# An S4 convolution and a PEER expert layer on one core: parameters in three parts, step sizes on chip, gelu for two head groups, and a new order

## The chip, the cores and the metric

The kernel runs on one core of a Trainium2 chip. A core has five engines with queues of their own: PE (TensorE, matrix products; its weight loads are shown as PEld), DVE (VectorE), ACT (ScalarE), POOL (GpSimd) and SP (SyncE, which here only issues DMAs). Engines work at the same time and wait for one another through semaphores; each runs its own instructions strictly in order. The metric is the device time of one execution in microseconds (us); the median of several runs counts.

## The reference, cut to what matters

```python
xn = layernorm(x)                                  # x: 1 x 2048 x 448, no affine part
out = x + s4(xn) + peer(xn)

def s4(u):                                         # 448 channels, 256 states each
    dt = exp(log_dt)[:, None]
    A, B, C = A_re + 1j*A_im, B_re + 1j*B_im, C_re + 1j*C_im
    P = exp((dt * A)[:, :, None] * arange(2048))
    K = einsum("dn,dnl,dn->dl", C, P, dt * B).real # a filter of 2048 taps for each channel
    return causal_convolution(u, K) + u * Dskip    # by FFT in the reference

def peer(x):                                       # 16 heads, 64 x 64 = 4096 experts
    q = einsum("nd,dhc->nhc", x, w_q)              # two halves of 256 for each head
    s1, s2 = q[..., :256] @ k1.T, q[..., 256:] @ k2.T
    e = 64 * argmax(s1) + argmax(s2)               # top 1 of each half
    g = softmax(top score over one candidate)
    return sum over heads of g * gelu(x . u[e]) * v[e]
```

## The kernel before

**The work.** The 2048 tokens are 16 tiles of 128. Four kinds of work have no data in common until the end, and run beside each other:

- *Parameters* (`params`, and `exp32` for the step sizes). `exp32` computes dt = exp(log_dt) in 19 DVE operations on a tile of 112x4; the result goes to memory (`dt_d`) and comes back broadcast to 128 partitions. `params` takes six tables (real and imaginary parts of A, B and C, states on the partitions, 2 x 448 columns = 896) and makes from them, for each channel and state, a log magnitude and a phase, as tables of exponents and of integer phase steps. Both tables go to memory (`tt_d`, `tp_d`) and are loaded back for four batches at a time (`exponents`, `steps`). It is a chain of 36 DVE operations on 128x896, four on POOL, and some on ACT (sine, square, logarithm, exponential) between them.
- *The filter* (`batch`, `products`): 56 batches of 8 channels. For each, PE makes exponents (lg, L579), ACT exponentiates them (mg, L590), DVE makes phases (ph, L610 and L614), ACT takes sines and cosines (CS, L629 to L635), DVE multiplies (zi and mg, L660 to L666), PE sums over the states (kp, L682). After each quarter of the channels `conv` convolves the tokens with the filter by matmuls and leaves the result in memory (t_d).
- *The router* (`combine`, `ln`, `score`). `combine` multiplies w_q with the keys (32 loads wq, products wc, L862, transposed by wt, L875). `ln` normalizes the tiles (L915 to L921), transposes them (xtp, L943) and projects them (up, L724). `score` makes for each tile and four groups of heads the scores in PSUM (sc, L961 and L970, banks of the pool s2), reduces them to the maximum (mx, L985, DVE, 64 of these), finds its position and writes the indices ig.
- *The experts* (`experts`): for each tile four groups of 4 heads of 32 tokens x 4. POOL gathers rows of u and v (ue, L1083, four gathers for a group), DVE takes dot products with the token (L1091), and a chain between ACT and DVE makes gelu: square (ACT, L1098), x (DVE, L1101), dw (DVE, L1110), tanh (ACT, L1104), th (DVE, L1107), and A, the 32-column selector times th (DVE, L1114). PE adds up v rows with A (po, L1121). There are 64 such chains. `final` adds everything into the output (L1167).

**What sets the order.** Nothing is scheduled by a planner: the string `ORDER` has a character for each step of each stream (`CODE` maps characters to streams), and steps are emitted in that order; each engine's queue is what falls to it. Buffers are rings: gathers, wq loads and scratch tiles share the ring `q` ("ue", eleven of them), score banks are "s2", po has one bank.

## Time and profile before

| | us |
|---|---|
| three runs | 761.42, 763.97, 760.34 |
| median | 761.42 |
| profiled execution | 763.02 |
| its span, first to last instruction | 761.1 |
| ACT busy | 552.9 |
| POOL busy | 360.7 |

The profile is of one execution. Busy times are of instructions that compute; issuing a DMA or waiting is not among them. A row of the timeline has the start, the duration, the engine, the line, the operation, the tile written and those read, the shapes, and in brackets the idle time before it with what ended that. A group of instructions has busy time, the mean in ns, and the idle time before its members. Waits are listed as the engine, the tile and line, what was waited for, the total in us, the count and the longest one. An operation's duration includes a tail that the next one on the engine overlaps, so cost is better read from the distance between starts.

Three more things of the trace of before are needed to follow the next part. The first reduction of scores that has a filter product behind it, the 17th, starts at 134.70 us. The last one starts at 357.95, and the last product of the filter ends near 714.6.

### The profile page before, as it was taken

The page shows a single profiled execution, that of the slowest core. Times are in us where ns is not written, and L with a number is a line of the kernel's source. Part 1 is how long each engine was busy: PE and PEld are TensorE (multiplying, and loading weights), DVE is VectorE, ACT ScalarE, POOL GpSimd, SP SyncE. Part 2 cuts the span into 40 slices and gives each one's busy share as a digit, 9 for nine tenths or more (in the row PEclk, how much of TensorE's full clock was granted, in tenths as well). Part 3 has the DMA queues.
Part 4 walks back from the last instruction along what each step waited for, and adds up shares of the span by engine and source line. Part 5 has one row for each costly group of instructions (what it writes and reads, how often), then busy time and mean ns, then how long its engine had stood idle before and what let it go on. Part 6 is the DMA issues. An engine that isn't in the chain of part 4 may idle for free.

```text
span 761.1 us, 19861 instructions
## 1 busy us (share of the span) xinstructions
PE 652.1 (86%) x7628; PEld 355.8 (47%) x7628; DVE 669.5 (88%) x1691; ACT 552.9 (73%) x1137; POOL 360.7 (47%) x307
## 2 busy tenths in 40 slices
PE   1999999999999999999887958679996587899882
PEld 0344333443444444444465734346763344576751
DVE  4896578999999999999999999999998999999840
ACT  3886147566876886774796898888898888999630
POOL 2011024544363645655447686484564657752523
PEclk9999999999999999999999877688987756999995
DMA  9998656978687896887989999899898999977998
GB/s 324 328 374 305 228 136 254 355 238 246 221 257 266 252 327 191 309 255 257 337 300 340 281 324 361 263 327 279 265 342 271 308 325 286 339 248 209 296 178 128
DMA packets 119095, 211.83 MB, mean 278 GB/s; under 512 B 38937, under 2 KB 94233, under 8 KB 118937
## 3 DMA queue, kind: packets, MB, share of 16 engines
q0 software_dynamic: 31232, 124.80, 51.6%
q1 hardware_dynamic: 87768, 85.77, 35.2%
q8 instruction: 60, 0.98, 0.5%
q14 instruction: 35, 0.28, 0.1%
HBM read 180.90 MB, written 33.29 MB: 281 GB/s over the span
## 4 chain that ended last, share of the span: by engine, by line
PE 41%; DVE 29%; ACT 14%; DMA 7%; issue 6%; SPq 1%; POOL 1%; POOLq 0%; DVEq 0%; ACTq 0%
PE sc L961 14%; DVE ue L1091 6%; PE U L798 3%; PE po L1121 3%; DVE mg L666 3%; DVE zi L662 3%; DVE ph L614 3%; PE kp L682 3%; PE sc L970 3%; DMA ue<-in_uv_dram,ig 3%; PE ip L830 2%; PE wc L862 2%; PE up L724 2%; ACT CS L629 2%; DMA VU<-vu_d 2%
## 5 line engine op out<-in xcount | busy, mean ns | idle before, releaser
L1083 POOL DMA_INDIRECT ue<-in_uv_dram,ig x256 | 312.6, 1221 | 309.0 <-PE po L1121 72.9
L961 PE MATMUL sc<-W,xt 128*128 128x512 f32 x384 | 180.1, 608 | 2.2 <-ACT xt L946 1.9
L1091 DVE SCALAR_TENSOR_TENSOR ue<-ue,xr 128x448 f32<-128x448 f32 x256 | 154.1, 617 | 4.0 <-DMA ue<-in_uv_dram,ig 4.0
L961 PEld LDWEIGHTS sc<-W,xt 128*128 128x128 f32 x384 | 69.7, 191 | 91.9 <-issue 83.9
L1121 PE MATMUL po<-ue,A 128*32 128x448 f32 x512 | 68.6, 616 | 9.4 <-DVE A L1114 5.0
L590 ACT ACTIVATE mg<-lg 128x512 f32<-128x512 f32 x112 | 63.4, 600 | 11.1 <-PE lg L579 10.6
L682 PE MATMUL kp<-mg 128*32 128x64 f32 x1792 | 62.3, 237 | 7.9 <-DVE kt L693 3.1
L666 DVE TENSOR_TENSOR mg<-mg,CS 128x1024 f32<-128x1024 f32 x56 | 68.2, 1217 | 0.0
L662 DVE TENSOR_TENSOR zi<-mg,CS 128x1024 f32<-128x1024 f32 x56 | 68.2, 1217 | 0.0
L635 ACT ACTIVATE CS<-CS,halfpi 128x1024 f32<-128x1024 f32 x56 | 64.5, 1152 | 0.8
L614 DVE CUSTOM_DVE_ANT_0 ph<-st,ph 128x512 uint16<-128x512 uint16 (+2 forms) x84 | 64.9, 772 | 0.2
L629 ACT ACTIVATE CS<-ph 128x1024 f32<-128x1024 int32 x56 | 62.6, 1118 | 1.4 <-issue 0.5
L632 ACT ACTIVATE CS<-ph 128x1024 f32<-128x1024 int32 x56 | 63.2, 1128 | 0.0
L682 PE MATMUL kp<-zi 128*32 128x64 f32 x1792 | 61.6, 234 | 0.0
L682 PEld LDWEIGHTS kp<-mg 128*32 128x32 f32 x1792 | 45.2, 119 | 29.2 <-issue 11.7
L579 PE MATMUL lg<-lc,rt 32*128 32x512 f32 x112 | 39.8, 548 | 21.5 <-ACT mg L590 17.5
L702 PE MATMUL vp<-f,kt 128*64 128x128 f32 x448 | 43.6, 326 | 16.5 <-ACT tl L1163 5.0
L985 DVE TENSOR_REDUCE mx<-sc 128x8 f32<-128x512 f32 x64 | 43.6, 682 | 14.6 <-PE sc L970 9.2
L682 PEld LDWEIGHTS kp<-zi 128*32 128x32 f32 x1792 | 47.2, 121 | 0.1
L798 PE MATMUL U<-VU,g 128*64 128x128 f32 x384 | 42.3, 301 | 5.4 <-DVE cp L808 2.7
L702 PEld LDWEIGHTS vp<-f,kt 128*64 128x64 f32 x448 | 28.9, 160 | 38.3 <-issue 11.9
L862 PE MATMUL wc<-wq,kk 128*64 128x448 f32 x128 | 31.7, 586 | 17.1 <-DMA wq<-in_wq_dram 17.1
(244 smaller groups left out, 1242.2 us busy)
## 6 DMA issues: line engine op xcount, KB each, us to landing
wq<-in_wq_dram SPq DMA_DIRECT2D x32, 448.0 KB
xr<-xn_d SPq DMA_DIRECT2D x64, 224.0 KB
vu_d<-vst SPq DMA_DIRECT2D x64, 112.0 KB
VU<-vu_d SPq DMA_DIRECT2D x12, 512.0 KB
t_d<-tq SPq DMA_DIRECT2D x24, 256.0 KB
tl<-t_d SPq DMA_DIRECT2D x12, 512.0 KB
ue<-in_uv_dram,ig POOLq DMA_INDIRECT x256, 6.4
xx<-in_x_dram SPq DMA_DIRECT2D x16, 224.0 KB
```

What stands on the lines that cost most here:

```text
L614: s.nc.vector.tensor_tensor(out=rw(n, 2 * n), in0=rw(0, n), in1=o["st"][:, k, b0:b0 + 2].rearrange("p b h m x -> p (b h m x)")[:, None].to ...
L629: s.nc.scalar.activation(CS[:, 1].rearrange("p (m r x) -> p m r x", r=16, x=2), four(s.ph), AF.Sin, scale=SC)
L635: s.nc.scalar.activation(B["CS"][:, 0], B["CS"][:, 0], AF.Sin, scale=-SC, bias=s.halfpi)
L662: V.tensor_tensor(out=zi[:, 512:], in0=mg[:, 512:], in1=CS[:, 1], op=ALU.mult)
L666: V.tensor_tensor(out=mg[:, 512:], in0=mg[:, 512:], in1=CS[:, 0], op=ALU.mult)
L682: s.nc.tensor.matmul(kp[32 * c:32 * c + 32, 64 * gi:64 * gi + 64], T[ri][:, 1024 + m:1056 + m], view(T[ri], m, [[512, 2], [1, 32]]), start ...
L702: s.nc.tensor.matmul(vp[64 * ri:64 * ri + 64, 128 * gi:128 * gi + 128], B["kt"][:, 64 * gi:64 * gi + 64], s.f1[:, ri], start=True, stop=True)
L798: s.nc.tensor.matmul(U[64 * h:64 * h + 64, sl, ri], s.g[q][:, 2 * kk + h, ri], src[:, k1 + h, :w], start=True, stop=True)
L961: s.nc.tensor.matmul(B["sc", q].rearrange("p a b -> p (a b)"), B["xt"][:, i], w, start=(q % 2 == 0 and i == 0), stop=(q % 2 == 1 and i == 2))
L1083: s.nc.gpsimd.indirect_dma_start(out=ue, out_offset=None, in_=s.io["uv"], in_offset=bass.IndirectOffsetOnAxis(ap=s.IDX[t][:, c, g:g + 1].b ...
L1091: s.nc.vector.scalar_tensor_tensor(Q["ue", c][:, :D], Q["ue", c][:, :D], 1.0, B["xr", c], op0=ALU.mult, op1=ALU.mult, accum_out=Q["dot"][: ...
L1121: s.nc.tensor.matmul(B["po"][32 * c:32 * c + 32, :D], Q["A"][:, c], Q["ue", c][:, D:], start=(g == 0), stop=(g == 3))
```

## The change

Four things change; what is computed stays the same.

1. **Parameters in three parts of channels**, 128, 160 and 160 wide (`PARTS`): 256, 320 and 320 columns where there were 896. Each part has two packed loads (tiles pa and pb) and takes its buffers from the ring `q`. The first part's tables stay on chip: the exponents are transposed straight from the tile pt, and the steps are read from the tile pb (`P["R1"]`). Parts two and three go through memory as before.
2. **Step sizes without memory.** log_dt is broadcast to 128 partitions by its first load, and `exp32` works on 128x448 into the tile `s.dt`, which stays.
3. **Gelu for two groups at once** from tile 4 on (`PT=4`): the tiles x, th and dw become 128x8 and A 128x256, and the four operations of DVE and two of ACT serve eight gathers. 16 + 24 chains take the place of 64.
4. **A new order string**; the mask is loaded later, the DMA scratch is 2048, not 4096.

```diff
+PARTS = (128, 160, 160)
...
 ORDER = (
-    "4HH4HH44441444Z4444H606HH414144114H72III2II72II2I2I7728I8I2IJJ22I2I2I2I72KIZ414I82852I24K4I4COP224C4234LMLDHMHHH4LMDCLM4"
...
+    "013ZHH3HH314Z3353153H33116633HH3H322I2222I2I2II2I2III222I2222I7IJJI3K7IICI7788I2IIL8DC332699I798M7874I77OC8DEC77778I7I9D"
...
-            T["ld"] = s.sm.tile([112, 4], F32, name="ld")
-            s.nc.sync.dma_start(T["ld"], io["log_dt"].rearrange("(p f) -> p f", f=4))
-        x = p.add("c_ld", "SP", xf(112, 16), ldt)
-        ops = s.exp32(T)
-        x = p.chain("c_v", "DVE", ops, deps=[x])
-        x = p.add("dt_st", "SP", xf(112, 16), lambda: s.nc.sync.dma_start(s.dt_d.rearrange("o (p f) -> (o p) f", f=4), T["p"]), deps=[x])
...
+            v, w = s.flat("q", "dq", 1024), s.flat("q", "dr", 1024)
+            T.update(ld=v[:, :D], k=v[:, D:2 * D], r=w[:, :D], ki=w[:, D:2 * D].bitcast(I32), p=s.dt)
+            s.nc.sync.dma_start(T["ld"], io["log_dt"].rearrange("(o f) -> o f", o=1).to_broadcast([128, D]))
+        x = p.add("c_ld", "SP", xf(128, 1792), ldt, take=("ue", "ue"))
+        s.dt_done = p.chain("c_v", "DVE", s.exp32(T), deps=[x], give=("ue", "ue"))
...
-    def params(s, part):
+    def params(s, k):
...
-        N = 2 * D
...
+        d0, w = s.parts[k]
+        N, nb, b0 = 2 * w, w // NB, d0 // NB
+        per = 1024 // N
+        keep = k == 0
...
+        P["tp_done"] = [c1] if keep else [stp(0, 0, "A_re", [f2]), stp(0, 1, "T3", [ph]), stp(1, 0, "B_im", [f1]), stp(1, 1, "T1", [c1])]
...
+                s.nc.tensor.transpose(o["ps"][:, t], P["tt"][t][:, i:i + 4].rearrange("p b k -> p (b k)") if P["keep"] else o["tl"][:, t], s.ident)
...
+            if P["keep"]:
+                o["tp"] = P["R1"][:, :, :, i:i + 4]
...
-        for g in range(4):
+        w = 2 if t >= s.o["PT"] else 1
+        for g0 in range(0, 4, w):
...
+                            for k in ("dot", "x2", "th", "dw"):
+                                Q[k] = s.sm.tile([128, 2, 4], F32, name=k, bufs=2)[:, :w]
...
+                A = Q["A"] = s.sm.tile([128, 2, 4, 32], F32, name="A", bufs=2)[:, :w]
+                s.nc.vector.tensor_tensor(out=A.rearrange("p g c k -> p (g c) k"), in0=s.mask[:, None, :].to_broadcast([128, 4 * w, 32]),
+                                          in1=Q["th"].rearrange("p g c -> p (g c)")[:, :, None].to_broadcast([128, 4 * w, 32]), op=ALU.mult)
...
-    nc = bacc.Bacc("TRN2", target_bir_lowering=False, num_devices=1, dynamic_dma_scratch_size=4096)
+    nc = bacc.Bacc("TRN2", target_bir_lowering=False, num_devices=1, dynamic_dma_scratch_size=2048)
```

In what follows a row is one instruction of an engine's queue: line, operation, tile written and tiles read, shape. The changed kernel's lines are about ten higher: mx is L995, wc is L872, up is L734.

DVE before, the end of the parameter chain around the first reduction of scores (mx); pv, pw, px and pz are parameter tiles, ISA is an integer addition:

```order
L496 TENSOR_SCALAR pv<-pw 128x896
L985 TENSOR_REDUCE mx<-sc 128x8
L921 TENSOR_TENSOR q<-m,y 128x2
L497 ISA px<-pw,pv 128x1792
L498 TENSOR_SCALAR pw<-pw 128x896
L992 TENSOR_TENSOR eq<-sc,mx 128x512
L499 ISA pw<-pw 128x1792
```

DVE now, at the first and second reductions of scores; pa, pb and pt are the tiles of the second part:

```order
L995 TENSOR_REDUCE mx<-sc 128x8
L1002 TENSOR_TENSOR eq<-sc,mx 128x512
L470 RECIPROCAL pb<-pb 128x320
L995 TENSOR_REDUCE mx<-sc 128x8
L433 TENSOR_TENSOR pa<-pa,pb 128x320
L462 TENSOR_TENSOR pt<-pb,pt 128x20x8
L433 TENSOR_TENSOR pa<-pa 128x320
L439 SCALAR_TENSOR_TENSOR pa<-pa 128x320
```

Before, all but the last five of the 36 operations of the chain stand ahead of the first reduction. Now the second part's chain stands among them, and the third part's is further on; it ends here, right ahead of the 17th reduction (the ISA rows are its phase tables, L1103 is a dot product):

```order
L496 TENSOR_SCALAR pb<-pb 128x320
L497 ISA pb<-pb 128x640
L1103 SCALAR_TENSOR_TENSOR ue,dot<-ue,xr 128x448
L928 TENSOR_TENSOR q<-y 128x2
L1013 TENSOR_TENSOR eq<-eq 128x32x16
L929 SCALAR_TENSOR_TENSOR q<-q,v 128x2
L1013 TENSOR_TENSOR eq<-eq 128x32x8
L498 TENSOR_SCALAR pb<-pb 128x320
L1016 TENSOR_REDUCE cm<-eq 128x32
L499 ISA pt<-pt,pb 128x640
```

Between the 16th and the 17th reduction stand 52 rows in all.

PE's first rows before (wt are transposes of wc, xtp of a normalized tile, up the projection of tiles):

```order
L862 MATMUL wc<-wq,kk 64x448 x4
L943 MATMUL xtp<-ident,xx 128x128 x4
L943 MATMUL xtp<-ident,xx 64x128
L862 MATMUL wc<-wq,kk 64x448 x4
L724 MATMUL up<-xx,f_92 128x448 x3
```

and now:

```order
L872 MATMUL wc<-wq,kk 64x448 x4
L734 MATMUL up<-xx,f_91 128x448
L872 MATMUL wc<-wq,kk 64x448 x4
L953 MATMUL xtp<-ident,xx 128x128 x4
L953 MATMUL xtp<-ident,xx 64x128
```

The first up has moved ahead of the first transposes, and three in a row have become single ones between the wc.

DVE's first rows now, where the step sizes (dq, dr, dt) and the first tile's layer norm (v, y, q) alternate:

```order
L355 TENSOR_SCALAR dq<-dq 128x448
L358 TENSOR_SCALAR dq<-dq 128x448
L925 TENSOR_SCALAR v<-s 128x2
L359 TENSOR_SCALAR dq<-dq 128x448
L362 SCALAR_TENSOR_TENSOR dr<-dq 128x448
L362 SCALAR_TENSOR_TENSOR dr<-dq,dr 128x448
L358 TENSOR_SCALAR dt<-dr 128x448
L926 TENSOR_SCALAR y<-v 128x2
```

Before, the same operations stood there on 112x4, between parameter operations on 128x896.

More of the change, by code (lines that the diff above doesn't have):

```diff
@@ L425, in params @@
+        held = 3 if keep else 4
+        l1 = p.add("par_ld", "SP", xf(128, 4 * N * per), ld1, take=("ue",))
+        l2 = p.add("par_ld", "SP", xf(128, 4 * N * (6 - per)), ld2, take=("ue",) * (held - 1))
         d1, d2 = dv(N), dv(N, 2)
@@ L513, in exponents @@
-    def exponents(s, g):
+        P["tt_done"] = [ll] if keep else [p.add("par_st", "SP", xf(128, 128 * nb), lambda t=t: s.nc.sync.dma_start(
+            s.tt_d[:, t, b0:b0 + nb], P["tt"][t]), deps=[ll]) for t in range(2)]
+        p.add("par_f", "NONE", 0, lambda: None, deps=[ph, lf, an, ll, f1, c1] + P["tp_done"] + P["tt_done"],
+              give=("ue",) * (1 if keep else held))
+        return P
+    def exponents(s, P, g):
         p = s.p
         o = {}
+        i = 4 * g - P["b0"]
         def l():
```

287 lines of the change are left out of this document (140 added, 147 removed).

## The prediction

> **What bounds the kernel now.** I read the page's busy shares and slices first, then the windows by stage. Of the slices I show VectorE (DVE) and the clock that TensorE (PE) was granted.
>
> ```profile
> PE 652.1 (86%) x7628; PEld 355.8 (47%) x7628; DVE 669.5 (88%) x1691; ACT 552.9 (73%) x1137; POOL 360.7 (47%) x307
> DVE  4896578999999999999999999999998999999840
> PEclk9999999999999999999999877688987756999995
> PE 41%; DVE 29%; ACT 14%; DMA 7%; issue 6%; SPq 1%; POOL 1%; POOLq 0%; DVEq 0%; ACTq 0%
> ```
>
> PE and DVE are within 17 us of one another, and the chain of waits (fourth line) changes between them. An average cannot say which decides, so here are the stages that I cut: up to PE's first work, up to its last starved piece, the parameters' two halves (the fourth stretch ends with the 17th reduction of the scores, the first that has products behind it), and the long middle to the last product, then the end.
>
> ```profile
> core 0: us, PE busy (x) PEld busy (x) DVE busy (x) ACT busy (x) POOL busy (x), PEclk, DMA share, GB/s
> 0.00:16.40 16.40, 0.00 (x0) 0.01 (x1) 6.92 (x9) 6.79 (x17) 4.77 (x17) 1.00 0.89 314
> 16.40:30.20 13.80, 11.34 (x27) 3.47 (x27) 11.98 (x41) 10.55 (x17) 0.00 (x0) 1.00 0.94 320
> 30.20:62.70 32.50, 32.32 (x155) 13.44 (x156) 30.14 (x37) 24.61 (x63) 5.14 (x2) 1.00 1.01 368
> 62.70:134.70 72.00, 70.10 (x230) 28.43 (x226) 46.97 (x110) 33.70 (x94) 15.39 (x14) 1.00 0.66 223
> 134.70:358.60 223.90, 221.63 (x1755) 96.97 (x1748) 219.25 (x595) 157.21 (x351) 111.65 (x94) 1.00 0.80 263
> 358.60:714.60 356.00, 289.80 (x4907) 193.86 (x4906) 341.42 (x860) 308.75 (x565) 211.69 (x172) 0.85 0.94 301
> 714.60:761.10 46.50, 26.90 (x574) 19.62 (x569) 12.78 (x46) 11.30 (x33) 12.06 (x10) 0.78 0.90 177
> ```
>
> From 134.7 to 714.6 DVE is busy 219.25 + 341.42 = 560.7 of 579.9 us (97%), and PE 511.4 (88%). So DVE bounds the middle: what it loses ahead of 134.7 is not made up later, and DVE work taken out of the middle comes off whole. Ahead of 134.7 DVE has slack: its idle time in the first four stretches is 9.5 + 1.8 + 2.4 + 25.0 = 38.7 us, and there PE sets the pace (70.1 of 72.0). The scores come through PE, and the DVE queue's own waits from 62.7 to 134.7 say so:
>
> ```profile
> DVE mx L985 <- PE sc L970: 8.6, 2, 4.4
> DVE mx L985 <- PE sc L961: 5.1, 5, 1.4
> ```
>
> The change touches that slack, and the gelu chains in the middle.
>
> **Term 1, the head: step sizes and parameters.** The prices come from DVE's timeline and groups:
>
> ```profile
> 17.22 1.08 DVE L432 TENSOR_TENSOR pw<-pw 128x896 f32<-128x896 f32 x1
> 18.22 1.08 DVE L432 TENSOR_TENSOR pw<-pw,px 128x896 f32<-128x896 f32 x1
> 132.24 0.15 DVE L1101 SCALAR_TENSOR_TENSOR x<-x,dot 128x4 f32<-128x4 f32 x1
> 132.31 0.16 DVE L1110 TENSOR_TENSOR dw<-dot,ig 128x4 f32<-128x4 f32 x1
> L435 DVE TENSOR_SCALAR pv<-pv 128x896 f32<-128x896 f32 x2 | 1.2, 623 | 0.0
> ```
>
> Back to back, 896 columns take 18.22 − 17.22 = 1.00 us and 4 columns 132.31 − 132.24 = 0.07 us. So an operation costs 0.07 us plus 1.04 ns a column; one with a single tensor operand (623 ns less the 0.08 overlap is 0.54) costs about half as much a column.
>
> - Step sizes: 19 operations on 112x4 become 19 on 128x448. Ten are TENSOR_SCALAR: 0.07 + 448 x 0.52 ns = 0.30 us; nine have two tensors: 0.54. The sum is 3.0 + 4.8 = 7.8, against 19 x 0.07 = 1.3: +6.5 us. The store and reload of dt vanish, two small transfers, and nobody on the path stood behind them.
> - Parameters: 256 + 320 + 320 columns are the same 896, but 36 DVE operations become 105: 69 more by 0.07 is +4.8 us.
> - Position: pricing every DVE row ahead of the 17th reduction in the two orders this way, the changed one has 10.3 us more: 6.5 + 4.8, less 1.0 of dot products and layer norm that now come later.
> - Idle: parameters used to fill the start, where DVE waits for PE anyway. Now a first part runs ahead of the first reduction, 21.9 us of work in all, and the scores for it are there at about 48 (PE's time up to then in its own row lengths), so about 24 idle; then about 10 more up to the second, whose scores PE has some 13 us later. That is 33.4 us against 38.7, −5.3.
> - Port: a POOL operation of the parameters held DVE up.
>
> ```profile
> 41.81 2.36 POOL L432 TENSOR_TENSOR pv<-pv,dt 128x896 f32<-128x896 f32 x1 [26.85 <-DMA dt<-dt_d]
> 42.15 2.05 DVE L918 TENSOR_TENSOR q<-y 128x2 f32<-128x2 f32 x1
> ```
>
> A two-column operation took 2.05 us, against about 0.15, until the POOL operation ended. Four such POOL operations become twelve of a third of the width: the same columns, about 9 to 10 us of POOL in all. If none falls on a DVE row −8 us, if all do +2; four operations of 2 us did before, and twelve short ones fall partly into idle stretches: −1.
>
> Rule beside the row: the Trainium skill, "SBUF — State Buffer", section "Who interferes with whom", says that the pair of ports between VectorE and GpSimd is an exclusive lock held for a whole instruction, so the loser is blocked fully. The 2.05 us row agrees. By the rule the twelve would all count where DVE has work, the +2 end, and the forecast would be 3 us later.
>
> DVE alone thus gives 10.3 − 5.3 − 1 = **+4.0** at the 17th reduction. PE alone gives a gain:
>
> ```profile
> 16.42 1.72 PE L862 MATMUL wc<-wq,kk 128*64 128x448 f32 x2 [16.42 <-DMA wq<-in_wq_dram]
> 22.01 1.33 PE L943 MATMUL xtp<-ident,xx 128*128 128x128 f32 x5
> 25.96 1.02 PE L724 MATMUL up<-xx,f 128*128 128x448 f32 x2 [0.48 <-ACT xt L946]
> 30.22 1.72 PE L862 MATMUL wc<-wq,kk 128*64 128x448 f32 x8
> ```
>
> Unstarved, eight wc take 1.72 us (fourth row); at the start two took as long. In 16.4 to 30.2 stand 16 wc (3.4 us), 5 transposes (1.3) and 6 up (3.1), 7.8 us in 13.8: 6.0 us starved. In SP's order 4.1 MB stood ahead of the first wq, now 3.0 MB; at 314 GB/s that is 3.4 us earlier. With half of the 6.0 saved too (up is spread between wc, but the first up needs the first tile's layer norm, which now queues among 17 of the 128x448 operations), PE alone gives −6.4. PE's matmuls are the same 7628, and in the order the first kp stands behind the same 83 score matmuls and the last score behind the same 96 po in both. PE therefore moves with its start alone, and I take the DVE end, because 20 us of DVE work now stand between the 16th and 17th reductions, part three among it, and PE has three score banks to run ahead in before it waits too.
>
> **Term 2, gelu for two groups.** 64 chains become 16 + 24 = 40. Each merge drops three 4-column operations (x, th, dw) and one fixed part of A: 4 x 0.07 = 0.28 us; 24 of them −**6.7 us** of DVE. ACT also drops 48 operations of about 0.2 us, which lie beside DVE's work. The waits in the middle:
>
> ```profile
> L1098 ACT ACTIVATE x<-dot 128x4 f32<-128x4 f32 x64 | 13.2, 207 | 13.9 <-DVE ue L1091 13.8
> DVE x L1101 <- ACT x L1098: 4.6, 6, 2.7
> DVE th L1107 <- ACT th L1104: 2.4, 4, 1.2
> ```
>
> 4.6 + 2.4 = 7.0 us of DVE waits for the chain's round trips. With 24 of 64 trips gone by count 2.6 go; a pair with two groups' dot products ahead of it has more to run meanwhile: **−3.0** (bounds 0 and −7.0).
>
> **What costs nothing.** Loads and stores of the tables for part one are spared (16 of 56 batches), covered either way by a DMA share of 0.66 in 62.7 to 134.7. The later mask load and the smaller DMA scratch I put at nothing: no A is needed ahead of the 17th reduction, and the gathers' price is POOL's, at 47%. More ACT table switches (62 become 72) lie under ACT's 33.7 of 72 us busy there:
>
> ```profile
> L477 ACT ACT_TABLE_LOAD x1 | 1.3, 1283 | 0.0
> ```
>
> Ten would be 12.8 us were that cover gone. The end, 714.6 to 761.1, has the same instructions: 46.5.
>
> **Sum.** 763.02 (the profiled execution: a span of 761.1 and 1.9 around it) + 4.0 − 6.7 − 3.0 = 757.3. The median of the runs, 761.42, is 1.6 under that execution: 755.7, so **756 us**. A measurement here can tell about 0.5%, 3.8 us: faster is under 757.6, slower over 765.2.
>
> **The rivals.**
>
> R1, slower: the parameter chain's round trips to ACT, paid three times. One chain waits for ACT like this now:
>
> ```profile
> DVE px L432 <- ACT px L481: 2.1, 1, 2.1
> DVE px L435 <- ACT pw L450: 1.6, 1, 1.6
> DVE pz L465 <- ACT pz L462: 3.1, 2, 2.7
> ```
>
> That is 6.8 us, in a stretch where DVE idles anyway. Parts two and three have the same trips, between reductions that PE then waits for: every mx queued behind them is late, then its bank. Twice 6.8 is +13.6, giving 769. For it: 20 us of DVE between two reductions, and ACT's queue there also holds the score copies. Against it: the order puts score work between the operations of a part. It turns the forecast into slower once 9.5 us of these 13.6 are exposed.
>
> R2, no change: the pairs give back what they save. A pair holds eight gather tiles, not four, until its po:
>
> ```profile
> L1083 POOL DMA_INDIRECT ue<-in_uv_dram,ig x256 | 312.6, 1221 | 309.0 <-PE po L1121 72.9
> ue<-in_uv_dram,ig POOLq DMA_INDIRECT x256, 6.4
> L1091 DVE SCALAR_TENSOR_TENSOR ue<-ue,xr 128x448 f32<-128x448 f32 x256 | 154.1, 617 | 4.0 <-DMA ue<-in_uv_dram,ig 4.0
> ```
>
> POOL already waits 72.9 us for po to free them, and a gather lands 6.4 us after its issue, so with fewer tiles free the next dot waits. One microsecond for a quarter of the 24 pairs cancels the 6.7: 762. Against it: DVE's idle time ahead of the 256 dot products is only 4.0 us for gathers now.
>
> R3, faster by more: PE's start decides, −6.4 in place of +4.0, giving 745. For it: PE is 99% busy from 62.7 to 358.6. Against it: the 20 us.
>
> R4, it doesn't do what it says: the first part kept on chip is to free the products sooner, but they stand behind the same 83 score matmuls. That is in the sum, which books nothing for it.
>
> **Numbers.** Forecast .43, own range 751 to 761; R1 .22; R2 .20; R3 .15. The range 745 to 769 takes both ends of the head and of the waits. Faster: R3 .15 and most of the forecast, .36, is .51; slower: R1 .22 and the tails of R2 .05, .27; the rest .22.
>
> **What would show it.** Step 1: the 17th reduction at about 139 in place of 134.7, with DVE busy over 100 us up to there; earlier than 131 is R3, over 146 with waits for ACT in the parameter lines is R1. Step 2: 40 chains, and x and th waits under 5 us; dot products waiting for gathers over 6 us are R2. The first wc should start near 13. My number is wrong if the head moves one way and the middle gives it back: the stretch from the 17th reduction to the last product (579.9) should shrink by about 10.

## The result and the profile after

The changed kernel takes 793.12 us (median of runs from 791.18 to 796.40). The kernel before took 762.69 us beside it on the same chip. The ratio is 1.0402, with a 95% interval of 1.0349 to 1.0455: 4.0% slower, where 0.7% faster was forecast and nothing over 769 was in the range.

The profiled execution has a span of 794.3 us against 761.1, so 33.2 us are to be found. Four instants, the same in both kernels, cut that into pieces (starts in us; the last reduction of scores ahead of the products is the 16th, the first behind which products run is the 17th; a product is here DVE's last multiplication of a batch, on the tile mg, L666 before and L676 now):

| | before | changed | later by |
|---|---|---|---|
| 16th reduction (mx) | 126.29 | 127.27 | 1.0 |
| 17th reduction | 134.70 | 148.96 | 14.3 |
| first product of the filter on DVE | 144.6 | 157.5 | 12.9 |
| last such product | 712.4 | 735.1 | 22.7 |
| end of the span | 761.1 | 794.3 | 33.2 |

So the head loses 12.9 us, the stretch from the first to the last product 9.8, and the tail behind it 10.5. (The description of the kernel before calls the reduction at 357.95 the last; it is the 61st of 64, and the 64th starts at 376.8. No number of the forecast rests on it.)

The page of the changed kernel, busy shares and two rows of slices:

```profile
PE 649.5 (82%) x7628; PEld 358.4 (45%) x7628; DVE 670.8 (84%) x1667; ACT 565.2 (71%) x1121; POOL 369.0 (46%) x315
DVE  5705989999999999999999989989979979998510
PEclk9999998799999999999998959679886966999975
```

No engine has 33 us more to do: DVE is busy 670.8 us against 669.5, PE 649.5 against 652.1, ACT 565.2 against 552.9. So engines wait. DVE's slices (19.9 us each) show a hole at 40 to 79 us (0 and 5) and a long thin end. The clock that PE was granted dips in the seventh and eighth slice, 119 to 159 us, where it stood at full speed before: PE was starved there.

Now the head alone, by windows. The columns are the window and its length, then busy time (with the count of instructions) of each engine, the clock, the DMA share and GB/s; the last row adds the windows up. The changed kernel up to its 17th reduction:

```profile
0.00:62.70 62.70, 44.22 (x189) 17.14 (x190) 27.97 (x79) 38.40 (x98) 4.35 (x19) 1.00 0.93 320
62.70:126.00 63.30, 59.33 (x187) 24.80 (x185) 53.20 (x122) 32.47 (x89) 14.35 (x13) 1.00 0.53 179
126.00:148.96 22.96, 12.06 (x33) 4.00 (x34) 22.62 (x66) 22.09 (x37) 10.39 (x10) 0.70 0.53 153
sum 148.96, PE 115.61 PEld 45.93 DVE 103.79 ACT 92.97 POOL 29.09; mean PE 38.54 PEld 15.31 DVE 34.60 ACT 30.99 POOL 9.70
```

The kernel before, up to its own:

```profile
0.00:62.70 62.70, 43.66 (x181) 16.92 (x183) 49.04 (x85) 41.95 (x96) 9.91 (x19) 1.00 0.96 343
62.70:126.00 63.30, 61.40 (x193) 25.26 (x190) 39.27 (x84) 27.57 (x77) 9.17 (x9) 1.00 0.67 228
126.00:134.70 8.70, 8.70 (x38) 3.17 (x36) 7.70 (x27) 6.13 (x18) 6.23 (x5) 1.00 0.59 182
sum 134.70, PE 113.76 PEld 45.35 DVE 96.01 ACT 75.66 POOL 25.31; mean PE 37.92 PEld 15.12 DVE 32.00 ACT 25.22 POOL 8.44
```

DVE did 103.79 us of work up to the 17th reduction instead of 96.01, +7.8. Its idle time is 148.96 − 103.79 = 45.2 us instead of 38.7, +6.5. Together that is the 14.3. DVE has 21.1 us less work in the first window, 13.9 more in the second and 14.9 more in the third. The third window is the one to look at: PE, which filled it before (8.70 of 8.70), works 12.06 of 22.96 us there, while DVE (22.62) and ACT (22.09) are both full.

The middle, by DVE's own waits from 134.7 to 714.6, in the changed kernel (waiting tile and line, what it waited for, total us, times, longest):

```profile
DVE ue L1103 <- DMA ue<-in_uv_dram,ig: 9.9, 4, 5.5
DVE kt L703 <- ACT kt L700: 6.5, 7, 2.0
DVE x L1113 <- ACT x L1110: 4.9, 4, 4.2
...
DVE th L1119 <- ACT th L1116: 2.0, 3, 1.3
```

and in the kernel before, behind the x and th rows that the prediction shows:

```profile
DVE ue L1091 <- DMA ue<-in_uv_dram,ig: 2.0, 2, 1.0
DVE kt L693 <- ACT kt L690: 1.8, 3, 0.9
```

x and th waits stay at 6.9 us (7.0 before). The dot products wait 9.9 us for gathers instead of 2.0, and kt (the filter's cast) 6.5 for ACT instead of 1.8.

The tail, on POOL: the last stores of the convolution to the output (tl), in the changed kernel:

```profile
781.04 1.29 POOL L1178 DMA_DIRECT2D out_dram<-tl  x1 [3.51 <-issue]
785.08 1.27 POOL L1178 DMA_DIRECT2D out_dram<-tl  x1 [2.76 <-issue]
789.16 1.29 POOL L1178 DMA_DIRECT2D out_dram<-tl  x1 [2.80 <-issue]
```

and before:

```profile
754.16 1.27 POOL L1167 DMA_DIRECT2D out_dram<-tl  x1 [3.73 <-ACT tl L1163]
756.01 1.29 POOL L1167 DMA_DIRECT2D out_dram<-tl  x1 [0.57 <-ACT tl L1163]
```

Before, a store waits for ACT to make its tile, and two go out 1.85 us apart. Now the last three stand 4.04 and 4.08 us apart, and what ends the wait is "issue": no engine and no semaphore that the profile shows. The page's chain of waits, followed back from the end, stops there too, after 2% of the span:

```profile
issue 2%; POOL 0%; POOLq 0%; DMA 0%
```

That is the one place where a piece of the loss has a face of its own, so it was tried first.

### The profile page after: what moved, and what is told of

Its sections match the earlier page's. It is cut to its first block, busy times and chain, and to the rows that moved or that the text cites. A ratio compares the mean times of both kernels' runs of the same rounds, so it can differ in the third digit from the quotient of the medians.

```text
span 794.3 us, 19828 instructions
## 1 busy us (share of the span) xinstructions
PE 649.5 (82%) x7628; PEld 358.4 (45%) x7628; DVE 670.8 (84%) x1667; ACT 565.2 (71%) x1121; POOL 369.0 (46%) x315
## 5 line engine op out<-in xcount | busy, mean ns | idle before, releaser
L1095 POOL DMA_INDIRECT ue<-in_uv_dram,ig x256 | 316.1, 1235 | 268.5 <-PE po L1138 84.4
L1103 DVE SCALAR_TENSOR_TENSOR ue<-ue,xr 128x448 f32<-128x448 f32 x256 | 153.1, 619 | 9.9 <-DMA ue<-in_uv_dram,ig 9.9
L692 PE MATMUL kp<-mg 128*32 128x64 f32 x1792 | 64.9, 241 | 26.7 <-DVE mg L676 14.6
L600 ACT ACTIVATE mg<-lg 128x512 f32<-128x512 f32 x112 | 62.7, 599 | 16.4 <-PE lg L589 16.1
L692 PEld LDWEIGHTS kp<-mg 128*32 128x32 f32 x1792 | 47.1, 122 | 49.1 <-issue 16.9
L676 DVE TENSOR_TENSOR mg<-mg,CS 128x1024 f32<-128x1024 f32 x56 | 68.1, 1216 | 0.0
L692 PE MATMUL kp<-zi 128*32 128x64 f32 x1792 | 64.8, 239 | 2.7 <-issue 2.7
L645 ACT ACTIVATE CS<-CS,halfpi 128x1024 f32<-128x1024 f32 x56 | 64.5, 1151 | 1.0
L995 DVE TENSOR_REDUCE mx<-sc 128x8 f32<-128x512 f32 x64 | 43.6, 681 | 20.9 <-PE sc L980 18.8
L692 PEld LDWEIGHTS kp<-zi 128*32 128x32 f32 x1792 | 49.0, 124 | 3.2 <-issue 3.2
L840 PE MATMUL ip<-cp,e 64*128 64x256 f32 x384 | 46.5, 394 | 0.0
L1178 POOL DMA_DIRECT2D out_dram<-tl x16 | 22.1, 1381 | 49.8 <-issue 19.4
L712 PE MATMUL vp<-f,kt 128*64 128x128 f32 x448 | 38.9, 305 | 5.6 <-ACT VK L716 1.7
L589 PEld LDWEIGHTS lg<-lc,rt 32*128 32x128 f32 x112 | 15.6, 195 | 60.9 <-ACT mg L600 31.9
```

What stands on the lines that cost most here:

```text
L600: s.nc.scalar.activation(mg[:, :2, i], ps.rearrange("p (k n) -> p k n", k=2), AF.Exp)
L645: s.nc.scalar.activation(B["CS"][:, 0], B["CS"][:, 0], AF.Sin, scale=-SC, bias=s.halfpi)
L676: V.tensor_tensor(out=mg[:, 512:], in0=mg[:, 512:], in1=CS[:, 0], op=ALU.mult)
L692: s.nc.tensor.matmul(kp[32 * c:32 * c + 32, 64 * gi:64 * gi + 64], T[ri][:, 1024 + m:1056 + m], view(T[ri], m, [[512, 2], [1, 32]]), start ...
L1095: s.nc.gpsimd.indirect_dma_start(out=ue, out_offset=None, in_=s.io["uv"], in_offset=bass.IndirectOffsetOnAxis(ap=s.IDX[t][:, c, g:g + 1].b ...
L1103: s.nc.vector.scalar_tensor_tensor(Q["ue", g, c][:, :D], Q["ue", g, c][:, :D], 1.0, B["xr", c], op0=ALU.mult, op1=ALU.mult, accum_out=Q["d ...
```

## The experiments

Where a kernel is said to be "the changed kernel with scratch 4096", it is e1, which was run four times under different labels as the companion of others. Two of the chips took 833 and 843 us for the kernel before itself; what ran there is read by its ratio, or against a companion on the same chip.

| run | what it is | us | before beside it | ratio (95%) |
|---|---|---|---|---|
| e1 | change, scratch 4096 | 780.48 | 763.55 | 1.0253 (1.0170 to 1.0336) |
| e2 | before, scratch 2048 | 785.20 | 763.55 | 1.0297 (1.0226 to 1.0367) |
| e3 | e1, gelu of pairs taken apart | 787.06 | 763.55 | 1.0311 (1.0240 to 1.0383) |
| e4 | e1, step sizes on 4 columns | 777.98 | 763.55 | 1.0203 (1.0117 to 1.0288) |
| g1 | e1, third part without DVE | 779.08 | 766.04 | 1.0226 (1.0146 to 1.0305) |
| g2 | e1 again | 777.52 | 766.04 | 1.0186 (1.0122 to 1.0249) |
| h1 | e1, third part without ACT tables | 779.84 | 764.72 | 1.0219 (1.0158 to 1.0280) |
| h2 | both, g1 and h1 | 772.27 | 764.72 | 1.0115 (1.0052 to 1.0177) |
| h3 | e1 again | 780.72 | 764.72 | 1.0212 (1.0152 to 1.0272) |
| e5 | e1, second and third part earlier | 850.54 | 832.95 | 1.0253 (1.0176 to 1.0330) |
| e6 | e1, third part late, scratch 3456 | 856.43 | 832.95 | 1.0297 (1.0218 to 1.0376) |
| e8 | e1, second early and third late, scratch 3456 | 852.46 | 832.95 | 1.0249 (1.0173 to 1.0326) |
| f1 | e1 again | 851.07 | 842.78 | 1.0137 (1.0064 to 1.0210) |
| f2 | e6 again | 860.75 | 842.78 | 1.0223 (1.0165 to 1.0280) |
| b7 | before, pairs from tile 4, scratch 3840 | 839.65 | 832.95 | 1.0127 (1.0081 to 1.0172) |
| b8 | before, pairs from tile 6, scratch 3840 | 841.12 | 842.78 | 0.9919 (0.9866 to 0.9972) |
| b9 | before, pairs from tile 10, scratch 3840 | 844.16 | 842.78 | 0.9992 (0.9941 to 1.0044) |
| g3 | b8 again | 779.68 | 766.04 | 1.0214 (1.0166 to 1.0262) |

### The scratch (e1, e2)

e1 gives the changed kernel the scratch that the kernel before has. That takes room on chip which the new tiles hold, so dt lies in another tile's buffer and the tanh is written over x; neither adds an operation.

```diff
-        s.dt = c.tile([128, D], F32, name="dt")
+            s.dt = s.flat("vk", "dt", 4096)[:, :D]
...
-                s.nc.scalar.activation(Q["th"], Q["x2"], AF.Tanh, scale=math.sqrt(2 / math.pi) * 0.044715)
+                s.nc.scalar.activation(Q["x2"], Q["x2"], AF.Tanh, scale=math.sqrt(2 / math.pi) * 0.044715)
...
-    nc = bacc.Bacc("TRN2", target_bir_lowering=False, num_devices=1, dynamic_dma_scratch_size=2048)
+    nc = bacc.Bacc("TRN2", target_bir_lowering=False, num_devices=1, dynamic_dma_scratch_size=4096)
```

> The changed kernel with the DMA scratch at 4096 again, as before the change; to make room on chip, the step sizes lie in the buffer of VK (free until then) and tanh is done in place. Theory S, the scratch: POOL's second store of a pair to the output waits until the first has landed (641.82 and 647.96 us in the changed kernel), the gathers behind it come late (DVE waits 5.5 us for one, 6.7 in the end), and the last stores are 4 us apart. Then the time falls from 793 to between 774 and 779, and the stretch from the last product to the end from 59 back to about 49. Rival P, the pairs of gelu hold the gather tiles: the time stays above 788.

e2 is the opposite: the kernel before, with nothing changed but this number.

```diff
-    nc = bacc.Bacc("TRN2", target_bir_lowering=False, num_devices=1, dynamic_dma_scratch_size=4096)
+    nc = bacc.Bacc("TRN2", target_bir_lowering=False, num_devices=1, dynamic_dma_scratch_size=2048)
```

> The kernel before with the scratch at 2048 and nothing else. Theory S: 762.7 becomes 772 to 780, with most of it after 640 us, where the stores stand. Rival P, the pairs (which this kernel doesn't have): within 3 us of 762.7.

Both moved, in opposite directions. e1 took 780.48 us, 12.6 less than the changed kernel, and missed its range by 1.5; e2 took 785.20, 21.7 more than the kernel before and 5 more than expected. e2 carries the proof, since it differs in one number. In e1 the head is the same (first product 157.6 for 157.5), the last product comes at 730.3 for 735.1, and the tail is 48.6 us, that of the kernel before (48.7). In the three other traces of e1 the tail is 48.7 to 50.0 us. POOL's last stores in e1, then in e2:

```profile
768.49 1.27 POOL L1178 DMA_DIRECT2D out_dram<-tl  x1 [0.29 <-ACT tl L1174]
771.93 2.57 POOL L1178 DMA_DIRECT2D out_dram<-tl  x2 [2.18 <-ACT tl L1174]
```

```profile
773.45 1.28 POOL L1167 DMA_DIRECT2D out_dram<-tl  x1 [2.86 <-issue]
777.53 1.29 POOL L1167 DMA_DIRECT2D out_dram<-tl  x1 [2.80 <-issue]
```

With 4096 a store waits for its tile, and the last two go out as one row of 2.57 us. With 2048 each waits for "issue", 4.1 us after the one ahead. The tiles of the changed kernel's last three stores had been ready for 7.7 to 10.8 us when these went out, those of e1's last three for 0.4 to 0.5. The 4.1 us are about how long such a store takes to land: of the changed kernel's page, 3.7 us from issue to landing in the median for the small ones, 5.8 for those of 256 KB. So the trace reads as if a second store were not issued until the first has landed. The large ones do the same in the middle, and POOL's queue also holds the gathers. The changed kernel around 640 us:

```profile
641.82 1.43 POOL L1178 DMA_DIRECT2D out_dram<-tl  x1 [0.36 <-issue]
647.96 1.31 POOL L1178 DMA_DIRECT2D out_dram<-tl  x1 [4.70 <-ACT x L1110]
649.57 1.09 POOL L1095 DMA_INDIRECT ue<-in_uv_dram,ig  x1 [0.30 <-PE vp L712]
```

and e1:

```profile
642.74 2.81 POOL L1178 DMA_DIRECT2D out_dram<-tl  x2
645.85 1.43 POOL L1095 DMA_INDIRECT ue<-in_uv_dram,ig  x1 [0.31 <-issue]
```

The second store goes out 6.1 us behind the first instead of right behind it, and the gather next in the queue is 3.7 us later. A dot product then waits for it:

```profile
655.06 0.68 DVE L1103 SCALAR_TENSOR_TENSOR ue<-ue,xr 128x448 f32<-128x448 f32 x1 [5.47 <-DMA ue<-in_uv_dram,ig]
```

(The row names ACT's x as what ended the 4.70; ACT had nothing to do with that store, whose tile was ready. Where the named releaser makes no sense, it was something the profile does not show.) So the scratch accounts for all 10.5 us of the tail and for 4.8 ahead of it, in these executions. The medians say 12.6, but the two kernels ran on different chips; the difference of their ratios says about 11.

### Gelu of pairs taken apart (e3)

e3 is e1 with each merged operation done twice, on half the tile; gathers, order and buffers stay.

```diff
-                s.nc.scalar.activation(Q["x2"], Q["dot"], AF.Square)
+                for k in range(w):
+                    s.nc.scalar.activation(Q["x2"][:, k], Q["dot"][:, k], AF.Square)
...
-                s.nc.vector.scalar_tensor_tensor(Q["x2"], Q["x2"], 1 / 0.044715, Q["dot"], op0=ALU.add, op1=ALU.mult)
+                for k in range(w):
+                    s.nc.vector.scalar_tensor_tensor(Q["x2"][:, k], Q["x2"][:, k], 1 / 0.044715, Q["dot"][:, k], op0=ALU.add, op1=ALU.mult)
```

> e1 with the six operations of a merged chain done once for each group, at the places where the merged ones stand, so order and waits are kept: 24 more of x, dw, th and A on DVE (6.7 us) and 48 more on ACT. If DVE's saved work comes off whole: 6 to 8 us over e1. Rival, the saved work had turned into waits: 0 to 2 us over e1.

787.06 us, 6.6 more than e1 on the same chip. The intervals of the two ratios overlap for the most part, so the medians alone do not settle the size. It is that of the forecast's 6.7. The place is not. The window of e1 from its first to its last product:

```profile
157.60:730.30 572.70, 492.06 (x6544) 284.73 (x6542) 544.94 (x1341) 456.89 (x860) 331.28 (x261) 0.91 0.90 285
```

and e3, with its tail:

```profile
157.90:732.20 574.30, 494.00 (x6546) 285.35 (x6544) 550.16 (x1429) 461.42 (x906) 336.42 (x261) 0.91 0.90 284
732.20:786.40 54.20, 30.39 (x648) 22.33 (x648) 14.54 (x50) 11.21 (x35) 11.31 (x9) 0.82 0.79 155
```

DVE does 5.2 us more work between the products in e3 (550.2 for 544.9), but the stretch grows by only 1.6: DVE's idle time falls from 27.8 to 24.1. The other 5.6 us appear in the tail, 54.2 for 48.6, where DVE works 14.5 of 54 and does not set the pace. There PE waits 11.7 us for the tile hl from memory, against 6.3 in e1 and 8.9 in g2, which is e1 again. No run ties that wait to the merges. So a microsecond of DVE work in the middle is not a microsecond of time there, and the 6.6 are not shown to be the saved work.

### Step sizes on four columns (e4)

```diff
+            s.nc.gpsimd.memset(s.dt, 0.018)
...
-            ops.append((dv(D, n), f))
+            ops.append((dv(4, n), f))
```

> e1 with the 19 operations of the step sizes on 4 columns in place of 448 (the other step sizes are a constant, so the convolution is not the reference's): takes 6.5 us of DVE work out of the first 30 us. Theory, DVE stands idle 16 us ahead of the first reduction and PE's start sets it: within 1.5 us of e1. Rival, my term of +6.5 us for them is on the path: 5 to 7 us under e1.

The 17th reduction comes at 146.44 for 149.06, 2.6 earlier, and the median is 2.5 lower, 777.98 (well inside the intervals of both; the instant in the trace is the better witness). That lies between the theory (within 1.5 us) and the rival (5 to 7). DVE's work up to there falls by 6.8 us, so the step sizes' +6.5 was sized well; 2.6 of it reach the 17th reduction, and the rest fits into DVE's hole of the first 60 us. The 2.6 are there at the first reduction already (49.51 for 52.15), and they come through PE: in e1 the first tile's layer norm ends on DVE at 19.3, between the wide step sizes, and PE's first up starts at 20.19 after a wait of 2.08 us; in e4 the norm ends at 14.7 and up starts at 18.48 without a wait.

### The head: what fills DVE and ACT ahead of the 17th reduction (g1, h1, h2)

Between the 16th and the 17th reduction lie 21.7 us now, 8.4 before. ACT's timeline of the changed kernel there (start, duration, line, operation):

```profile
134.18 1.28 ACT L477 ACT_TABLE_LOAD   x1
135.79 0.47 ACT L477 ACTIVATE pb<-pa 128x320 f32<-128x320 f32 x1 [0.33 <-DVE pa L433]
136.28 1.28 ACT L645 ACT_TABLE_LOAD   x1
...
138.74 1.28 ACT L480 ACT_TABLE_LOAD   x1
...
140.61 0.20 ACT L1110 ACTIVATE x<-dot 128x4 f32<-128x4 f32 x1
140.83 1.28 ACT L1116 ACT_TABLE_LOAD   x1
142.12 0.20 ACT L1116 ACTIVATE th<-x 128x4 f32<-128x4 f32 x1
```

The order has put the third part's functions (L477, L480), the first batch's cosines (L645) and a gelu's tanh (L1116) next to one another, and each needs another table. Eight table loads start from 126 to 149 us, 10.3 us in all; the kernel before has one there, at 137.32. And PE:

```profile
143.64 1.72 PE L1138 MATMUL po<-ue,A 128*32 128x448 f32 x8 [8.48 <-DVE A L1126]
145.29 4.92 PE L971 MATMUL sc<-W,xt 128*128 128x512 f32 x7
```

PE waits 8.48 us for A, which DVE makes from the tanh of 142.12; the scores for the 17th reduction stand behind this po in PE's queue. So PE's starvation begins on ACT's queue or on DVE's, which are both full. Three kernels take the third part's load off the one, the other, and both. g1 and h2 run without 31 of its 35 DVE operations, h1 and h2 with a plain copy in place of four of its functions (square root, arctangent, logarithm, exponential).

```diff
+        if k == 2:
+            for n in ("par_v", "par_v2"):
+                for st in p.streams[n][-len(p.streams[n]) // 3:]:
+                    if st not in lows:
+                        st.fn = lambda: None
```

> e1 without 31 of the 35 DVE operations of the third part's parameters (its tables are then not those of the reference; its loads, stores, POOL and ACT operations and the four differences of exponents remain): takes about 12 us of DVE work from right ahead of the 17th reduction. Theory, the place costs what its work is, and nothing behind it gives that back: the 17th reduction at 134 to 138 in place of 149, and 10 to 15 us under e1. Rival, something else holds the head or the middle (PE, the ring): less than 5 us under e1.

```diff
+        sq, at_, ln_, ex_ = (AF.Copy,) * 4 if k == 2 else (AF.Sqrt, AF.Arctan, AF.Ln, AF.Exp)
...
-        a3 = p.add("par_a", "ACT", ac(N), lambda: A.activation(B["C_im"], B["C_re"], AF.Sqrt), deps=[q], tset="Q")
+        a3 = p.add("par_a", "ACT", ac(N), lambda: A.activation(B["C_im"], B["C_re"], sq), deps=[q], tset="Q")
```

> e1 with the third part's square root, arctangent, logarithm and exponential on ACT replaced by copies (its tables are then not the reference's): no ACT table is loaded for them. In e1 ACT is busy without a gap from 126 to 150 us with eight table loads of 1.28 us between the third part's functions, the filter's and gelu's, and PE waits 7.6 us for an A whose tanh stands in that queue. Theory T+V, ACT's loads and DVE's operations of the third part each fill that stretch, so that taking one away alone gains little (g1 gained 2.4 us there): the 17th reduction 2 to 5 us earlier. Rival T, the table loads alone hold it: 8 to 12 us earlier, and 8 us or more under e1.

> g1 and h1 together: the third part without its 31 DVE operations and without its table loads (leaves both out). Theory T+V: now the 17th reduction comes at 132 to 138 in place of 149, and 8 to 14 us under e1. Rival, something else holds that stretch too (PE, the ring, the gathers): less than 6 us earlier.

The window from 126 to 150 us (busy PE, PEld, DVE, ACT, POOL) in h3, which is e1 again:

```profile
126.00:150.00 24.00, 13.93 (x34) 4.65 (x35) 23.64 (x68) 22.62 (x37) 10.71 (x10) 0.64 0.52 156
```

in g1, without the third part's DVE work:

```profile
126.00:150.00 24.00, 14.60 (x44) 5.05 (x44) 12.87 (x44) 22.46 (x38) 12.53 (x13) 0.79 0.72 219
```

in h1, without its tables:

```profile
126.00:150.00 24.00, 13.15 (x34) 4.57 (x35) 23.65 (x70) 14.96 (x31) 11.11 (x10) 0.72 0.54 161
```

and in h2, without either:

```profile
126.00:150.00 24.00, 18.23 (x61) 6.81 (x61) 18.47 (x57) 15.77 (x37) 14.10 (x14) 0.86 0.82 284
```

g1 halves DVE's load and leaves ACT full: the 17th reduction comes at 146.42, 2.4 us ahead of its companion g2. h1 takes 7.7 us from ACT and leaves DVE full: 149.08, 0.4 ahead of h3. h2 takes both: 140.19, 9.3 ahead, and 8.4 at the end (772.27 for 780.72). 2.4 and 0.4 apart, 9.3 together: two full engines side by side, and emptying one uncovers the other. PE's wait for that A says the same: 8.48 us in the changed kernel, 7.88 in g1, 8.47 in h1, 5.51 in h2. g1 and h1 each missed the place expected for the 17th reduction and gained nothing in time (779.08 against 777.52, 779.84 against 780.72); only the pair says why. h2's reduction is 2 us later than its range, its time is in it.

Why all of that work falls into this window is seen in SP's waits from 60 to 115 us of the changed kernel, and in its row that loads the third part:

```profile
SPq L1061 <- DVE pb L496: 24.6, 1, 24.6
```

```profile
108.39 0.41 SPq L402 DMA_DIRECT2D pa<-in_par_dram  x1
```

A store of expert indices (L1061) held SP's queue for 24.6 us while DVE came to it, and the loads of part three stand behind it. (The row names pb; the indices ix come from L1058, the DVE row ahead of that one, which ends at 102.42, and the store goes out at 102.45.) The chain can begin only at about 110, past most of the idle time (10.1 us from 62.7 to 126) that it could have filled. No run moved that store alone, so this is read from the trace and not tested.

### Parts in another place (e5, e6, f2, e8)

These rewrite the order string alone (e6, f2 and e8 also copy the third part's step sizes to a tile of their own, with a scratch of 3456). In e5 the second part follows the first directly and the third is loaded at 75.6 us; in e6 and f2 the third part's DVE work runs from about 400 to 495 us, where its batches are not yet due; e8 does both.

```diff
-    "3DP9I37J3ECLME83LFM9977C333D8ELHCMFLHFDHDF33ECDMFECFEEHFRLNJF33CDRMLD3E333CCKFEMLN33CDDFEN33337C33x55RDFECFDEDCFD7776667"
+    "3D55P9I37J3ECLME83LFM9977C83737D77EL6H7C3M7F7LH9F9DH7D8F89EC339D6MF6E7CF7E7EH7F8RL8N7JF8383C9D9RM6L8D39E7378C337CK9F7EM7"
...
+        s.dt2 = c.tile([128, PARTS[2]], F32, name="dt2")
```

> e1 with the second part's loads moved ahead on SP (behind the first 18 wq and tile loads) and its chain on DVE put right behind the first part's, ahead of the first reduction of scores, where DVE stood idle for 16.3 us; the third part takes the places that the second had. Theory H, the place of the parameters' DVE work costs the head: the 17th reduction, now at 149 us, comes at 134 to 139, and the time is 10 to 14 us under e1 (766 to 770). Rival W, the four tiles of the ring that it holds are taken from wq, PE starves and the first reduction comes after 60: no less than e1 minus 3.

> e1 with the third part's loads and chain moved behind the last scores (some 390 to 450 us), long ahead of its first use; its 160 step sizes are copied to a tile of their own, and the scratch is 3456 to make room for it. Theory M, DVE has slack in the middle that waits fill (24 more gelu operations, 6.7 us, moved the last product by only 1.9): the 17th reduction comes at 134 to 138 and 8 to 13 us of that are kept at the end (767 to 772). Rival D, as predicted, DVE bounds the middle, the 13 us are only moved: within 3 us of e1 (778 to 783).

> e5 and e6 together: the second part ahead of the first reduction, the third behind the last scores. With H and M: 17th reduction at 122 to 128, where PE's own pace sets it, and 756 to 763. With H and D: as e5. With W: as e6 or slower.

> e6 again, beside e1 on one chip. On the slow chip its first product came at 144.6 us, where the kernel before has it, but fell behind from there. Theory M (DVE has slack in the middle): 8 to 13 us under e1. Rival D (DVE bounds the middle, the third part's work is only moved): within 3 us of e1. Rival D2, it is worse than moved, since the four tiles that it holds are taken from the gathers: 4 us or more over e1.

e5 shows the cost of a chain that has nothing between its steps. Its first reduction starts at 74.9 us instead of 52.1, and the first product at 165.2. DVE's waits in e5 from 16 to 78 us:

```profile
DVE pt L462 <- ACT pt L459: 10.5, 3, 6.4
DVE pa L433 <- ACT pa L481: 4.2, 2, 2.6
DVE pa L433 <- ACT pa L448: 2.7, 1, 2.7
DVE pb L436 <- ACT pa L451: 2.0, 1, 2.0
```

19.4 us of waiting for ACT, with the reductions queued behind: the rival R1 in pure form, in a kernel that is not the changed one.

e6 and f2 bring the head back: 17th reduction at 136.11 and 137.01, first product at 144.6 and 145.8. Both are slower all the same. f2 and f1 ran on one chip, 860.75 against 851.07. From the first to the last product f2 takes 665.8 us and f1 635.4. DVE is busy 566.6 of it for 548.3 (+18.3, the third part), and idle 99.2 for 87.1 (+12.1). 6.9 us of the idle time are one wait of the moved chain for ACT (pa, L485). For gathers DVE waits 4.6 us instead of 0.8, so the expected cause, tiles taken from the gathers, is at most a small part. The smaller scratch shows no sign of its own: two of f2's large stores still go out 0.83 us apart (708.31 and 709.14). So 11.9 us won in the head cost 30.4 in the middle. e8 loses both ways (first product 151.3, last 798.1). None of these places for part three was cheaper than the one that the change has.

### Pairs in the old order (b7, b8, b9, g3)

The kernel before with the merged chains from tile 4, 6 or 10 on. The order string is rewritten where the merged steps stand (from tile 4 on a few gathers are later too), and the larger A takes its room from the scratch, 3840 instead of 4096, so these kernels do not differ in the merges alone.

```diff
+        w = 2 if t >= s.o["PT"] else 1
+        for g0 in range(0, 4, w):
```

> The kernel before with gelu for two groups at once and nothing else of the change: the merged operations stand where the second group's stood, both po behind them, a few gathers are later where no tile is free; scratch 3840 to make room for the larger A. If the merge is worth what e3 says: 755 to 758. Rival R2 of the prediction, eight gather tiles held for a pair cancel it in this order: 761 to 766, with DVE's waits for gathers and PE's for A longer by 5 or more.

> b7 with pairs from tile 6 on in place of tile 4: no gather has to be moved behind its old place. 20 merges, 5.6 us of DVE work. If b7 lost (1.3% over the kernel before) because pairs held gather tiles while the scores still run: now 3 to 8 us under the kernel before. Rival, pairs cost in any place of this order, because both groups wait for the second's gathers: no less than the kernel before.

> b7 with pairs from tile 10 on: 12 merges, 3.4 us of DVE work, all behind the last scores. By the first theory of b8: 2 to 5 us under the kernel before. By the rival: no less than it.

> b8 again, with more rounds: if it beats the kernel before by what b8 showed, 0.3 to 1.3% under it; if that was the slow chip alone, within 0.3%.

From tile 4 they are slower by 1.3% (1.0127). From tile 6 the first run looked like a version that beats both kernels, 0.9919, on a chip where the kernel before took 843 us. Run again where it takes 766, the same kernel is slower by 2.1% (1.0214): its last product is at 730.3 for 712.4. R2's sign is there: over the whole span dot products wait for gathers 11.9 us in g3 and 13.4 in b7, against 4.0 before; in b8 it is 6.0, in b9 2.0. In g3 DVE also waits longer for ACT at kt (7.7 us for 1.8), while its work between the products is 3.8 us less. So the tiles that a pair holds are a likely cause in b7 and g3, and the waits do not add up to all that was lost. The scratch does not look like the cause, since two of g3's stores go out 0.84 us apart (516.79 and 517.63), but no run has the pairs with 4096. From tile 10 there is no difference (0.9992). Why pairs from tile 6 help on one chip and hurt on another is open. No run here beats the kernel before on a chip of the usual speed.

The companions, which are e1 under other labels:

> e1 again, beside e6 on one chip, since e5, e6, e8 and b7 ran on a chip on which the kernel before took 833 us. On a chip where that takes about 763: 778 to 783.

> e1 once more, as the pair of g1 on the same chip: 1.4 to 2.5% over the kernel before.

> e1, as the pair of h1 and h2 on the same chip: 17th reduction at 149, 1.4 to 2.5% over the kernel before.

They came at 1.0137, 1.0186 and 1.0212, where the first run was at 1.0253. A difference between two of these kernels under some 5 us is therefore told by instants of the trace, not by the medians.

## Why the prediction was wrong, point by point

**"The smaller DMA scratch I put at nothing."** The miss with the clearest proof: 12.6 us in the changed kernel (e1), 21.7 in the kernel before (e2). The argument was that the gathers' price is POOL's and POOL is at 47%. But what the cut touches is not POOL's work; it is how many transfers of its queue can be under way at once, and at the end of the kernel POOL's stores are the path. No rival held this case.

**Term 1, "+4.0 at the 17th reduction".** It was +14.3. Of its parts, the work was about right: DVE's busy time rose by 7.8 where 10.3 − 1 was summed. The −1 for the port held: what DVE's rows beside a parameter operation of POOL take beyond the usual time of their shapes adds up to 6.0 us before and 5.0 now (before, one of the four POOL operations met hardly any DVE work, so the 8 us of the forecast's lower end were never there to be saved). The step that failed is the idle time, +6.5 for −5.3. The two stretches that were worked out came about as forecast: DVE idles 26.6 us up to the first reduction (about 24 were forecast) and 10.1 from there to the second (about 10). What was left out is that behind the second, up to 126 us, it idles another 8.1 us, since PE still sets the pace (59.33 of 63.3 busy from 62.7 to 126) and part three cannot start yet; its work then falls into a stretch without idle time.

A second step was wrong beside it, "more ACT table switches lie under ACT's 33.7 of 72 us busy". The ten loads came as counted (72 in all, 1283 ns each). The cover was an average over 72 us, and eight loads fell into 24 us in which ACT was full, beside a DVE that was full too. Alone this costs next to nothing: h1, without the third part's tables, has the 17th reduction 0.4 us earlier. It counts because it holds the place once DVE's work is gone (2.4 in g1). h2 gives 9.3 us of the 14.3 to the third part on both engines, and e4 gives 2.6 to the step sizes; if the two add, some 2.4 are left untraced. Taking tables or DVE work away alone shows little, which is why a price per engine could not see it. The Trainium skill, "ScalarE: Activation LUTs", section "What ACT_TABLE_LOAD costs", puts a switch at about 2.66 us with its drain; in this trace the tanh of 142.12 starts 1.29 us after its table load began, and that load 0.22 us after the operation ahead, so 1.3 us is what a switch took here.

**Term 2, "−6.7" for 24 merges.** The total fits, since e3 takes 6.6 more without them; as far as the traces go that is luck. "DVE work taken out of the middle comes off whole" was wrong: e3 has 5.2 us more work between the products and is 1.6 longer there; its other 5.6 stand in the tail, where PE waits for a load. A DVE at 97% was read as the bound; in e3 3.7 us of the added work went into DVE's idle time, so DVE is not the only engine that sets the pace.

**"−3.0" for x and th waits.** Nothing: 6.9 us for 7.0. There are fewer chains, and single waits are longer (4.2 us for 2.7).

**The end, "46.5".** With the scratch undone the tail is 48.6 for 48.7 (from the last product), so this held but for the scratch.

**The rivals.** R1 named the right chain, but as waits of DVE for ACT; in 126 to 149 us DVE does not wait at all (22.62 of 22.96 busy). Its price of 13.6 us is near what the head lost, for another reason, and its 769 lacked the scratch. Of R2's sign, dot products waiting for gathers over 6 us, the changed kernel has 9.9 and e1, with the same pairs, 5.4: 4.5 of it are the scratch. The other 3.4 above the kernel before may be the pairs; in the old order g3 has 11.9 with them (4.0 before). No run has the new order without pairs, so what they cost there by holding tiles is not shown, and R2 is not ruled out as a part of the middle's loss. R3: the first wc did start at 13.9 where 13 was forecast, and the first reduction 10.6 us earlier than before; by the 16th nothing was left of it (127.27 for 126.29). R4, the first part on chip frees no product sooner, was so.

**The sum.** Head 12.9, middle 9.8, tail 10.5. With the scratch undone (e1): 13.0, 4.9 and −0.1, for the 17.8 us by which e1's span exceeds that of the kernel before. The 4.9 are DVE's work −3.6 and its idle time +8.6; kt's wait for ACT is the largest row of e1 there (8.4 us against 1.8), and gathers are the next (5.4 against 2.0). No run took either wait away, so they are the most likely places, not shown ones; what in the new order makes ACT late for kt stays open.

## What to carry to other kernels

A cut that makes room (a smaller scratch, fewer buffers) costs nothing only if no two of the things that it holds need to be under way at once; look for that at the end of the program and in the queue that it shares, not in the engine's busy share. Check the cover of added work in the very stretch where the order puts it, on every engine that the moved chain uses, and together: two full engines side by side show little when either is relieved alone. In an order written out by hand an engine at 97% is not yet the bound; take a few operations away there and see whether the end moves.

## What was not expected of the hardware

With half the DMA scratch, POOL's stores to the output went out one landing apart, 4.0 to 4.1 us for 128 KB and 6.1 for 256 KB, where they had gone back to back (2.57 us for two); the page shows it only as "issue".

The same kernel (e1) took 778.9 us on one chip and 841.8 on another in the profiled executions, at mean granted clocks of 0.914 and 0.887:

```profile
core 0: 778.9 us, clock 0.914
```

```profile
core 0: 841.8 us, clock 0.887
```

Up to the first product the two agree within 0.2 us (157.6 and 157.7); the 8% come later. The clock is 3% lower, so it is not the clock alone. Between the products DVE's work is about the same (548.3 us for 544.9), its idle time 87.1 for 27.8; the rest is open. A kernel that gains on the one can lose on the other, as b8 and g3 do.
